# Two unused tiles ahead of the left-hand pools: a shift of SBUF addresses in a three-part attention, expert and convolution kernel

## The chip, the cores and the metric

The kernel runs on one core of a Trainium2 chip. The metric is the device time of one launch in microseconds. TensorE (PE) runs at one of two clock levels, 1.2 or 2.4 GHz; the profile gives the granted share of the higher one. All matrix products here are float32 data; the large ones use the float32r type, in which an operand is split into a high and a low part and a product is the sum of three (high by high, high by low, low by high).

## The reference

Three layers follow each other: a local and global attention, a mixture of experts whose expert is chosen per token (and may be held over from the token before), and a gated network with a three-tap convolution along the sequence.

```python
# attention, B=4, H=8, 512 local + 32 global tokens, head 64, window 32
s_g = scale * q_g @ k_all.T;  out_g = softmax(s_g) @ v_all
s_ll = where(|i - j| <= 32, scale * q_l @ k_l.T, -1e9)
out_l = softmax(concat(scale * q_l @ k_g.T, s_ll)) @ concat(v_g, v_l)
x = concat(out_g, out_l)            # (4, 544, 512)
# experts, E=8, D=512, F=1024
for b, s:
    e = argmax(x @ w_gate) if local_gate < 0.5 or s == 0 else prev_e
    out[b, s] = softmax(x @ w_gate)[e] * (relu(x[b, s] @ w1[e]) @ w2[e])
# second network
h = relu(x @ w_in)
conv_out = sum over k of conv_w[k] * h shifted by k - 1
y = (h * sigmoid(conv_out)) @ w_out
```

## The kernel before, in words

**Stages.** `Attn.run` computes the attention of the four batches (0 to about 150 us of the profile). `Routing` turns the gate logits into lists of tokens: each *slot* holds up to 128 tokens of one expert. `Moe.run` works through the slots (about 147 to 435 us): `gather` fetches the token rows (`xs`, [128, 512]) by an indirect DMA, `turn_x` transposes them and splits them into `xh` and `xl`, `layer1` multiplies them with the first weights, `turn_h` transposes the result and splits it into `gh` and `gl` ([128, 8, 128] each), `layer2` multiplies those with the second weights, and `scatter` writes the rows out. `Ffn2.run` is the second network (about 435 us to the end): 32 units of one batch and one 128-wide slice of the hidden layer, with the second product of a batch issued between the units of the next one, and that of the last batch at the very end.

**Which operand stands and which moves.** In the trace's names `out<-moving,stationary`. In the experts' first product (`l1_mm`, L1112) the token tile `xh` or `xl` is stationary (128 columns, loaded anew for each matmul) and the weights `wh` or `wl` move, 512 columns at a time. In the second (`l2_mm`, L1128) `gh` or `gl` is stationary and the second weights move, 512 columns. In the second network's first product (`l1_half`, L1546) it is the other way round: the weights stand, and the tokens (`f_x0h`/`f_x0l` for batches 0 and 2, `fxh`/`fxl` for 1 and 3) move, 272 columns. In its second (`Ffn2.l2_mm`, L1623) the hidden tile `fh` or `fl` stands and `w_out` moves, 512 columns, 256 in the last tile:

```python
for n, (x, w) in enumerate(((gh, wh), (gh, wl), (gl, wh))):
    self.nc.tensor.matmul(yp[:, cs], x[:, c], w[:, cs], ...)   # L1623: x stands, w moves
```

Every matmul has its own weight load (6066 of each in the profile). The next one's load runs beside the matmul before it.

**Where tiles lie.** SBUF tiles get their addresses in the order in which pools are opened. Pools open from the left (low addresses) unless they say `side="right"`. The first left pool is `const`, opened in `moe_kernel`; it holds `wz`, `ident`, `wcat`, `warm`, `L`, then the routing's tiles. All other left pools follow behind it, each at the place where the pool before it ends: the attention's, then `f_xp` (`fx`, `f_x0h`, `f_x0l`), `w_y` (`ws1`), `m_tp` (`ys`, `gh`, `gl`, `xh`, `xl`, `hs`, `xs`), `w_f` (`wf1`, `wf2`). When the experts are done, `Ffn2.open` opens `f_tp` where `w_y` began: three `f_hp` tiles, then `fxh`, `fxl`, `fc`, `fg`, `fh`, `fl`, `fy`. On the right lie the even batches' attention operands (`kT0`, `qT0`, `VA0`, `VB0`, `VC0`) and later the staging tile `ws2` and the split weights `wh`, `wl` of both layers (`w_hl`). Slots 0 and 1 are gathered before the attention ends, into a right-hand pool (`m_xa`), and slot 0's `xh` and `xl` lie there too.

No order table or planner is involved: the order of instructions is the order in which the code issues them, and it doesn't depend on addresses.

Of the kernel before, what the change touches and what calls it, by code (L numbers as in the profile page):

```python
# [8 lines left out]
F32 = mybir.dt.float32  # L9
# [8 lines left out]
P = 128  # L18
# [69 lines left out]
class Attn:  # L88
    def __init__(self, ctx, cr, cs, tc, q_l, k_l, v_l, q_g, k_g, v_g, wcat, wz, ident, x_dram, L, late, hook):
        self.tc, self.nc = tc, tc.nc  # L90
        nc = tc.nc
        self.q_l, self.k_l, self.v_l, self.q_g, self.k_g, self.v_g = q_l, k_l, v_l, q_g, k_g, v_g
        self.wcat, self.ident, self.x_dram, self.L, self.late, self.hook = wcat, ident, x_dram, L, late, hook
        self.lgt, self.wz = {}, wz
# [247 lines left out]
    def evac(self, c, ps, tag, w=P):  # L342
# [4 lines left out]
        if c < B:  # L347
            j = 4 * c + c // 2
            nc.vector.tensor_copy(self.L[:, j:j + 4, :], t.rearrange("p (i e) -> p i e", e=32)[:, :, 0:9])
        else:  # L350
            nc.vector.tensor_copy(self.L[0:w, 8, :], t[0:w, 0:9])

# [303 lines left out]
class Routing:  # L656
    def __init__(self, nc, c, pool, ident, L):
        self.nc, self.c, self.ident, self.L = nc, c, ident, L
        self.m = pool.tile([P, NT], F32, name="r_m")
# [277 lines left out]
    def few(self, b0, first):  # L937
# [3 lines left out]
        v.scalar_tensor_tensor(sm, b0, -128.0, first[0:1], ALU.mult, ALU.add)  # L941
        v.tensor_scalar(sm, sm, P - TS - 0.5, 1024.0, ALU.is_lt, ALU.mult)
        v.tensor_tensor(sm, sm, b0, ALU.add)
# [39 lines left out]
        v.tensor_tensor(self.gate, pg, rx, ALU.mult)  # L983


TS = 32
NTS = P // TS
NWARM_M = 10
# [66 lines left out]
class Moe:  # L1055
# [8 lines left out]
    def open(self, ctx):  # L1064
        self.ctx = ctx
        self.tp = ctx.enter_context(self.tc.tile_pool(name="m_tp", bufs=2))
        self.ps = ctx.enter_context(self.tc.tile_pool(name="m_ps", bufs=2, space=PSUM))
        self.ys = [self.tp.tile([P, DM], F32, name=f"ys{i}", bufs=1) for i in range(2)]
# [244 lines left out]
    def turn_x(self, s):  # L1313
# [13 lines left out]
        def raw():  # L1327
            nc.scalar.copy(xs[:, 0:NKC * TS].rearrange("p (k t) -> p k t", t=TS), t[:, :, P - TS:P])

# [11 lines left out]
    def layer1(self, s):  # L1341
# [4 lines left out]
        def few():  # L1346
            w = FF // NTS
            for k in range(NKC):
                for j in range(NTS):
                    nc.tensor.matmul(hp[0][TS * j:TS * j + TS, 0:w], xs[:, TS * k:TS * k + TS], W.s[1][:, k, w * j:w * j + w],  # L1350
                                     start=k == 0, stop=k == NKC - 1)
# [31 lines left out]
    def layer2(self, s):  # L1383
# [5 lines left out]
        def few():  # L1389
            for k in range(NFC):  # L1390
                j, a = divmod(k, n)
                for i in range(NTS):
                    nc.tensor.matmul(yp[TS * i:TS * i + TS, 0:w], hs[:, P * (n + a) + TS * j:P * (n + a) + TS * j + TS],
                                     W.s[2][:, k, w * i:w * i + w], start=k == 0, stop=k == NFC - 1)
            for i in range(NTS):
                nc.scalar.copy(y[P - TS:P, w * i:w * i + w], yp[TS * i:TS * i + TS, 0:w])

# [52 lines left out]
class Ffn2:  # L1450
# [32 lines left out]
    def open(self, ctx):  # L1483
        nc, tc = self.nc, self.tc
        self.tp = ctx.enter_context(tc.tile_pool(name="f_tp", bufs=2, reuse_waits="tile"))
        self.ps = ctx.enter_context(tc.tile_pool(name="f_ps", bufs=2, space=PSUM, reuse_waits="tile"))
        self.hp = [self.tp.tile([P, S + 2], F32, name=f"f_hp{i}", bufs=1) for i in range(3)]
        for t in self.hp:
            nc.gpsimd.memset(t[:, 0:1], 0.0)
            nc.gpsimd.memset(t[:, S + 1:S + 2], 0.0)  # L1490
        self.n = 0
# [207 lines left out]
def moe_kernel(ctx, tc, q_l, k_l, v_l, q_g, k_g, v_g, w_gate, w_local, w1, w2, w_in, conv_w, w_out, out):  # L1699
    nc = tc.nc  # L1700
    outf = out.rearrange("b s d -> (b s) d")
    with tc.manual_schedule():
        cp = ctx.enter_context(tc.tile_pool(name="const", bufs=1))
# [8 lines left out]
        warm = cp.tile([P, 1], F32, name="warm")  # L1712
        nc.scalar.activation(warm, ident[:, 0:1], AF.Exp)
        L = cp.tile([P, NT, 9], F32, name="L")
        cc = Consts()

        def late():
# [142 lines left out]
```

## Time and profile before

| | us |
|---|---|
| three runs | 642.68, 645.39, 645.6 (median 645.39) |
| the profiled execution, its own time | 643.43 |
| its span, first to last instruction | 641.7 |
| mean granted clock | 0.984 |

| engine | busy us | share of the span | instructions |
|---|---|---|---|
| PE matmul | 585.6 | 91% | 6066 |
| PE weight load | 483.6 | 75% | 6066 |
| DVE | 415.3 | 65% | 870 |
| ACT | 319.3 | 50% | 634 |
| POOL | 171.3 | 27% | 226 |

DMA moved 90.57 MB. Busy time of PE counts a matmul from its start to its modelled end, which overlaps the next one's start; how fast matmuls follow each other is read from the starts in the timeline, or from a chain piece's length divided by its count.

### The profile page before, as it was taken

The page shows a single profiled execution, that of the slowest core. Times are in us where ns is not written, and L with a number is a line of the kernel's source. Part 1 is how long each engine was busy: PE and PEld are TensorE (multiplying, and loading weights), DVE is VectorE, ACT ScalarE, POOL GpSimd, SP SyncE. Part 2 cuts the span into 40 slices and gives each one's busy share as a digit, 9 for nine tenths or more (in the row PEclk, how much of TensorE's full clock was granted, in tenths as well). Part 3 has the DMA queues.
Part 4 walks back from the last instruction along what each step waited for, and adds up shares of the span by engine and source line. Part 5 has one row for each costly group of instructions (what it writes and reads, how often), then busy time and mean ns, then how long its engine had stood idle before and what let it go on. Part 6 is the DMA issues. An engine that isn't in the chain of part 4 may idle for free. (4 is left out here: it accounts for less than half of the span.)

```text
span 641.7 us, 16204 instructions
## 1 busy us (share of the span) xinstructions
PE 585.6 (91%) x6066; PEld 483.6 (75%) x6066; DVE 415.3 (65%) x870; ACT 319.3 (50%) x634; POOL 171.3 (27%) x226
## 2 busy tenths in 40 slices
PE   7888888888988999979989899978899999999997
PEld 6666666766666888758767678758898998998986
DVE  7867577866956857785596984586983293393340
ACT  4754555564225454552454643665864374363331
POOL 7664910042032223223224230100032132300100
PEclk8999899999999999999999999998899999999999
DMA  8999658658047666575275673123101201000001
GB/s 223 217 218 235 186 126 189 194 194 287 18 158 272 218 210 227 185 264 197 84 261 182 247 281 125 51 89 86 50 1 51 81 3 49 34 1 34 33 35 50
DMA packets 60644, 90.57 MB, mean 141 GB/s; under 512 B 25726, under 2 KB 34198, under 8 KB 60504
## 3 DMA queue, kind: packets, MB, share of 16 engines
q1 hardware_dynamic: 57016, 78.93, 39.7%
q0 software_dynamic: 3520, 10.23, 4.7%
q8 instruction: 64, 1.05, 0.7%
q14 instruction: 44, 0.36, 0.2%
HBM read 125.87 MB, written 15.79 MB: 221 GB/s over the span
## 5 line engine op out<-in xcount | busy, mean ns | idle before, releaser
L1565 DVE SCALAR_TENSOR_TENSOR fc<-f_hp,cw,fc 128x544 f32<-128x544 f32 (+2 forms) x66 | 51.7, 784 | 72.8 <-ACT fc L1563 71.4
L1048 DVE TENSOR_TENSOR wl<-ws,wh 128x512 fp32r<-128x512 f32 (+1 forms) x92 | 74.4, 871 | 14.1 <-ACT wh L1047 12.5
L1047 ACT CAST wh<-ws 128x512 fp32r<-128x512 f32 (+1 forms) x96 | 66.2, 768 | 5.7 <-DMA ws<-in_moe_w_dram 5.3
L1128 PE MATMUL yp<-wl,gh 128*128 128x512 f32 x144 | 57.5, 399 | 3.6 <-DVEq L1299 3.3
L1128 PE MATMUL yp<-wh,gh 128*128 128x512 f32 x144 | 59.2, 411 | 1.1 <-ACTq L1299 0.9
L1128 PE MATMUL yp<-wh,gl 128*128 128x512 f32 x144 | 57.2, 397 | 0.0
L1112 PE MATMUL hp<-wl,xh 128*128 128x512 f32 x144 | 48.6, 409 | 7.7 <-DVEq L1299 7.1
L1623 PE MATMUL f<-wh,fh 128*128 128x512 f32 (+1 forms) x144 | 55.4, 385 | 0.0
L1623 PE MATMUL f<-wl,fh 128*128 128x512 f32 (+1 forms) x144 | 55.1, 383 | 0.0
L1623 PE MATMUL f<-wh,fl 128*128 128x512 f32 (+1 forms) x144 | 55.1, 382 | 0.0
L1112 PE MATMUL hp<-wh,xh 128*128 128x512 f32 x144 | 50.2, 421 | 2.8 <-ACT wh L1047 2.7
L278 ACT ACTIVATE pr<-sp,nm 128x128 f32<-128x128 f32 x128 | 36.5, 374 | 26.2 <-DVE nm L275 26.2
L1276 ACT ACTIVATE hs<-hp 128x512 f32<-128x512 f32 x36 | 19.9, 595 | 59.4 <-PE hp L1112 59.3
L1020 POOL TENSOR_TENSOR wf<-wf,fx 128x512 int32<-128x512 int32 x16 | 20.8, 1300 | 103.1 <-DVE fx L1019 75.3
L1112 PE MATMUL hp<-wh,xl 128*128 128x512 f32 x144 | 47.8, 404 | 0.0
L1073 POOL DMA_INDIRECT xs<-x_dram,gidx x22 | 26.3, 1194 | 73.6 <-ACT pr L278 34.1
L1085 POOL DMA_INDIRECT y_dram<-ys,sidx x22 | 23.6, 1070 | 70.9 <-ACT ys L1401 31.9
L1112 PEld LDWEIGHTS hp<-wl,xh 128*128 128x128 f32 x144 | 27.4, 194 | 16.8 <-DVEq L1299 9.3
L1570 ACT ACTIVATE f_hp<-f 128x544 f32<-128x544 f32 x31 | 19.4, 624 | 35.9 <-PE f L1546 35.7
L1128 PEld LDWEIGHTS yp<-wl,gh 128*128 128x128 f32 x144 | 27.2, 189 | 10.4 <-DVEq L1299 4.2
L1105 DVE TENSOR_TENSOR gl<-hlp,gh 128x512 fp32r<-128x512 f32 x36 | 23.3, 686 | 18.0 <-ACT gh L1378 16.3
L1632 ACT COPY fy<-f 128x512 f32<-128x512 f32 (+1 forms) x18 | 10.1, 563 | 48.6 <-PE f L1623 48.6
(382 smaller groups left out, 1506.3 us busy)
## 6 DMA issues: line engine op xcount, KB each, us to landing
ws<-in_moe_w_dram SPq DMA_DIRECT2D x42, 2048.0 KB
fx<-y_dram SPq DMA_DIRECT2D x17, 256.0 KB
raw<-in_k_l_dram SPq DMA_DIRECT2D x16, 256.0 KB
x_dram<-x SPq DMA_DIRECT2D x16, 256.0 KB
fx<-in_moe_w_in_dram SPq DMA_DIRECT2D x8, 512.0 KB
fx<-in_moe_w_out_dram SPq DMA_DIRECT2D x8, 512.0 KB
out_dram<-fy SPq DMA_DIRECT2D x16, 256.0 KB
VA<-in_v_l_dram SPq DMA_DIRECT2D x20, 192.0 KB
```

Source lines behind the costliest of these rows:

```text
L278: nc.scalar.activation(pr[:, hp, :], sp[:, hp, :], AF.Exp, bias=nm[:, hp:hp + 1], scale=-1.0)
L1020: nc.gpsimd.tensor_tensor(a, a, lo, ALU.add)
L1047: (cp.tensor_copy if cp else self.nc.scalar.copy)(h, src[n][:, k, :])
L1048: eng.tensor_tensor(l, src[n][:, k, :], h.bitcast(F32), ALU.subtract)
L1073: self.nc.gpsimd.indirect_dma_start(out=xs, out_offset=None, in_=self.x_dram[0:n, :], in_offset=bass.IndirectOffsetOnAxis(ap=self.rt.gidx[ ...
L1085: self.nc.gpsimd.indirect_dma_start(out=self.y_dram[:, :], out_offset=bass.IndirectOffsetOnAxis(ap=self.rt.sidx[:, s:s + 1], axis=0), in_= ...
L1105: self.nc.vector.tensor_tensor(hl[1][:, a:a + 4], t, hl[0][:, a:a + 4].bitcast(F32), ALU.subtract)
L1112: self.nc.tensor.matmul(hp[c], a[:, k, :], b[:, 512 * c:512 * c + 512], start=k == 0 and m == 0, stop=k == NKC - 1 and m == 2)
L1128: self.nc.tensor.matmul(yp, a[:, k, :], b, start=k == 0 and m == 0, stop=k == NFC - 1 and m == 2)
L1276: self.nc.scalar.activation(hs[:, 512 * c:512 * c + 512], hp[c], AF.Relu)
L1565: nc.vector.scalar_tensor_tensor(c[:, a:b], hp[:, a + t:b + t], self.cw[:, t, f:f + 1], c[:, a:b], ALU.mult, ALU.add)
L1623: self.nc.tensor.matmul(yp[:, cs], x[:, c], w[:, cs], start=f == 0 and n == 0, stop=f == NFC - 1 and n == 2)
```

## The change

Two tiles are allocated that nothing reads or writes. `pad_c` (104 float32, 416 bytes in each partition) stands in the `const` pool behind `L`, so everything that comes after it on the left moves up by 416 bytes. `pad_f` (8 float32, 32 bytes) is the first tile of `f_tp`, so that pool's other tiles move up by 448. Nothing on the right moves, nor do `ident`, `wz`, `wcat`, `warm` and `L`.

```diff
+PAD_C, PAD_F = 104, 8
...
         self.ps = ctx.enter_context(tc.tile_pool(name="f_ps", bufs=2, space=PSUM, reuse_waits="tile"))
+        self.tp.tile([P, PAD_F], F32, name="pad_f", bufs=1)
         self.hp = [self.tp.tile([P, S + 2], F32, name=f"f_hp{i}", bufs=1) for i in range(3)]
...
         L = cp.tile([P, NT, 9], F32, name="L")
+        cp.tile([P, PAD_C], F32, name="pad_c")
```

The built program has the same instructions in the same order on every engine, with the same waits: only addresses differ. Starting addresses modulo 256, from the two built programs:

| tiles | before | after |
|---|---|---|
| `wh`, `wl` of both layers, `ws2`; `xs` of slots 0 and 1, slot 0's `xh`, `xl` | 224 | 224 |
| `xs`, `xh`, `xl` of the other slots; `gh`, `gl`, `hs`, `ys` of all | 64 | 224 |
| `ws1`, `wf1`, `wf2`, `fx`, `f_x0h`, `f_x0l` | 64 | 224 |
| `fxh`, `fxl`, `fh`, `fl`, `fy` | 32 | 224 |
| `fc`, `fg` (two buffers each) | 32, 160 | 224, 96 |
| `f_hp` (three) | 64, 224, 128 | 0, 160, 64 |
| attention, right: `kT0`, `qT0`, `VA0` / `VB0` / `VC0` | 192 / 128 / 32 | the same |
| attention, left: `kT1`, `qT1`, `VA1` / `VB1` / `VC1` | 32 / 224 / 128 | 192 / 128 / 32 |
| attention, left: `pr`, `pts` | 160 | 64 |
| `ident` | 128 | 128 |

The pieces of a tile that one matmul reads keep its residue, except in `f_x0` and `fx`: a row of their four is 2176 bytes, so an odd row lies 128 further, and the second half of 272 columns 64 further. Their eight pieces lie, seen from the weights that stand, at 96, 160, 224 and 32 (`f_x0`) and at 64, 128, 192 and 0 (`fx`) before; at 0, 64, 128 and 192 for both after. For the tiles that stand before the moving weights, the distance from the stationary tile to the weights is 160 (L1112 but for slot 0, L1128) and 192 (L1623) before, and 0 after.

## Rows read from the trace of the kernel before

**Rows 1.** Busy time by stretch: engines, granted clock, DMA share, GB/s.
```profile
core 0: us, PE busy (x) PEld busy (x) DVE busy (x) ACT busy (x) POOL busy (x), PEclk, DMA share, GB/s
30.00:60.00 30.00, 24.14 (x667) 19.14 (x671) 20.35 (x55) 15.15 (x42) 17.35 (x18) 1.00 0.89 220
...
220.00:260.00 40.00, 40.00 (x192) 32.71 (x191) 27.71 (x46) 18.41 (x32) 11.55 (x10) 1.00 0.53 185
260.00:300.00 40.00, 35.90 (x245) 27.93 (x243) 27.93 (x45) 17.47 (x33) 10.89 (x10) 0.96 0.67 237
```

**Rows 2.** The chain that ended last: start us, us, what (the second network).
```profile
481.61 3.02 PE f L1546 x24
...
493.73 5.59 PE f L1623 x24
...
521.49 2.99 PE f L1546 x24
...
609.82 27.86 PE f L1623 x144
```

**Rows 3.** PE's groups by line and form: count, busy us, mean ns.
```profile
L1128 PE MATMUL yp<-wh,gh 128*128 128x512 f32 x144 | 59.2, 411 | 1.1 <-ACTq L1299 0.9 <-ACT gh L1101 0.2
...
L1623 PE MATMUL f<-wh,fh 128*128 128x512 f32 x128 | 51.0, 398 | 0.0
...
L1112 PE MATMUL hp<-wh,xh 128*128 128x512 f32 x144 | 50.2, 421 | 2.8 <-ACT wh L1047 2.7
...
L1546 PE MATMUL f<-f_x0h,wh 128*128 128x272 f32 x128 | 28.9, 303 | 3.5 <-PEq L1199 3.5
...
L1623 PE MATMUL f<-wh,fh 128*128 128x256 f32 x16 | 4.4, 277 | 0.0
```

**Rows 4.** Timeline of PE, a later slot's second product after a break: start us, us.
```profile
245.04 0.39 PE L1128 MATMUL yp<-wl,gh 128*128 128x512 f32 x1
...
245.96 0.40 PE L1128 MATMUL yp<-wh,gl 128*128 128x512 f32 x1
...
249.95 0.40 PE L1128 MATMUL yp<-wl,gh 128*128 128x512 f32 x1
```

**Rows 5.** Timeline of PE, a stretch at the lower clock.
```profile
288.91 1.06 PE L1112 MATMUL hp<-wh,xl 128*128 128x512 f32 x2
289.76 1.06 PE L1112 MATMUL hp<-wh,xh 128*128 128x512 f32 x2
```

**Rows 6.** Timeline of PE, slot 0's first product, two runs without a break.
```profile
147.30 0.39 PE L1112 MATMUL hp<-wl,xh 128*128 128x512 f32 x1
...
148.22 0.39 PE L1112 MATMUL hp<-wh,xl 128*128 128x512 f32 x1
...
156.98 0.40 PE L1112 MATMUL hp<-wl,xh 128*128 128x512 f32 x1
...
157.91 0.40 PE L1112 MATMUL hp<-wh,xl 128*128 128x512 f32 x1
```

**Rows 7.** Timeline of PE, the last tile's matmuls of 256 columns.
```profile
632.17 0.28 PE L1623 MATMUL f<-wl,fh 128*128 128x256 f32 x1
...
633.99 0.28 PE L1623 MATMUL f<-wh,fl 128*128 128x256 f32 x1
```

**Rows 8.** DVE's groups by form, and min/median/max ns of the `ws` tile's instructions.
```profile
L1048 DVE TENSOR_TENSOR wl<-ws,wh 128x512 fp32r<-128x512 f32 x64 | 42.0, 718 | 7.1 <-ACT wh L1047 5.6 <-PE hp L1112 1.5
...
L1048 DVE TENSOR_TENSOR wl<-wf,wh 128x512 fp32r<-128x512 f32 x8 | 5.3, 690 | 2.8 <-ACT wh L1047 2.6
...
L1048 DVE TENSOR_TENSOR wl<-ws,wh x92: 676/686/1443, 150.8 to 423.8; 128x512 fp32r<-128x512 f32 x64, 128x1024 fp32r<-128x1024 f32 x28
```

**Rows 9.** PE's groups by form: the attention's products with V.
```profile
L300 PE MATMUL op<-VC,pts 128*32 128x65 f32 x384 | 21.5, 223 | 1.3 <-ACT pr L278 1.3
...
L300 PE MATMUL op<-VB,pts 128*32 128x65 f32 x320 | 21.2, 223 | 2.8 <-issue 2.7
```

## The prediction

> **What bounds the kernel now.** I read the stretches first. In the experts' stage a stretch such as 220 to 260 us has PE busy for all of its 40.00 us at a granted clock of 1.00, beside DVE at 27.71, ACT at 18.41 and DMA at 0.53 [rows 1]; in the attention, 30 to 60 us, PE is busy for 24.14 of 30.00 and DMA for 0.89 of the time [rows 1]. Then the chain that ended last: through the second network it consists of PE alone, pieces of 24 matmuls one behind the other, down to the last piece of 144 matmuls that takes 27.86 us [rows 2]. So from the experts on, the end moves with the time from one matmul's start to the next one's, which I call the step. The change adds no instruction and no wait; it can act only through what an instruction costs at another address, and above all through the step of the large matmuls.
>
> The step now. Second network, second product: 5.59 us for 24, so 233 ns for 512 columns [rows 2]. Experts, second product: 245.96 to 249.95 us holds 17 steps, 235 ns each [rows 4]; I use 234. At the lower clock, 1.2 GHz, two matmuls of 512 columns take 289.76 - 288.91 = 0.85 us, or 425 ns each, one column for each clock period [rows 5]. At 2.4 GHz the same would be half, 213 ns. So at full clock every large matmul is stretched by some 20 ns, about 10%, and it is this stretch that an address could act on. The Trainium skill (TensorE: Matmul & The Clock Gate, section on the 56 ns gap) gives a step of N / 2.4 + 2.5 ns, 215.7 for 512 columns. The trace doesn't agree: its step is 233 to 234 ns.
>
> **The change, part by part.** *Two allocations*: no instruction, 0 us.
>
> *Experts' products, stationary tile from distance 160 to distance 0.* L1112 and L1128 have three forms of 144 rows each, 864 matmuls [rows 3]; 24 of L1112 belong to slot 0, whose `xh` and `xl` already lie at distance 0. So 840 move. Slot 0 is the experiment that the kernel before holds by chance: where it runs without a break, four steps take 148.22 - 147.30 = 0.92 us (230 ns) and 157.91 - 156.98 = 0.93 us (232 ns) [rows 6]. A later slot's first four steps after a break, at distance 160, take 245.96 - 245.04 = 0.92 us, 230 ns [rows 4]. Like for like the two distances don't differ by more than the reading of 0.01 us in four steps, 2 to 3 ns. The other neighbour is L1623, distance 192, with its 233 against 234. I take 233 for distance 0, since it is the longer series: 840 x -1 ns = -0.8 us. Bounds: below, the least stretch that a full-clock row of this kind shows, the 256-column matmuls of the last tile, 633.99 - 632.17 = 1.82 us for 16, 114 ns, or 227.5 for 512 columns [rows 7]: -6.5 ns x 840 = -5.5 us. Above, the largest difference that two sets of addresses show in one line, the next item's 1%: +2.3 ns x 840 = +1.9 us.
>
> *Second network, second product, 192 to 0.* 384 matmuls of 512 columns and 48 of 256 (three forms of 128 and of 16) [rows 3]. I take no change, for slot 0's reason. Bounds: -5.5 ns x 384 = -2.1 us, and +2.3 x 384 = +0.9 us.
>
> *Second network, first product.* Six forms of 128 rows [rows 3], half with `f_x0`, half with `fx`. The pieces of `fx` lie at 64, 128, 192 and 0 from the weights and step 3.02 us / 24 = 126 ns; those of `f_x0` lie at odd multiples of 32 and step 2.99 / 24 = 124.6 ns [rows 2]. That is 1.25 ns, 1%. After the change both lie at multiples of 64. `fx` keeps its set: 0. `f_x0` should step like `fx`: 384 x 1.25 ns = +0.5 us. Bounds 0 and +0.5.
>
> *Everything else at a new address.* DVE's subtraction L1048 reads two SBUF tiles. With `ws2` and `wh` at equal residues (the rows with 512 columns) it takes 718 ns on the mean, but 676 at the least and 686 in the middle of all forms; with `wf2`, 96 bytes off, 690 [rows 8]. So equal residues cost nothing there, the mean being drawn up by a few long ones, and DVE has 12 us to spare in 40 [rows 1]. If each of the 12 `wf` subtractions lost 28 ns it would be 0.3 us. In the attention `pts` moves against `VA0`, `VB0`, `VC0`, not against `VA1`, `VB1`, `VC1`; the products with `VC` and `VB`, which lie at 32, 128 and 224, all take 223 ns on the mean [rows 9]. I cost it at 0; the cover is PE's own 6 us of idle time in 30 [rows 1], and without cover 1% of 24 us for each 30 us would be 1.2 us over the stage. Transfers into shifted tiles keep their size and number; DMA's idle half in the experts' stage covers them.
>
> Sum: -0.8 + 0 + 0.5 + 0 = -0.3 us. The profiled execution took 643.43 us (span 641.7), 2 us under the median of 645.39; the four times average 644.3. An unchanged kernel lands there, so the forecast is 644.3 - 0.3 = **644.0 us**. The sum on the profiled execution itself would be 643.1.
>
> **Rivals.** *The addresses matter fully (faster).* Two readers, the moving operand and the next weight load, get in each other's way, and equal residues keep them apart. For it: the stretch exists only at the higher clock, and it differs between 256 and 512 columns, so it isn't a fixed cost. Against it: slot 0. If the step fell to twice that of 256 columns, both bounds below together give 5.5 + 2.1 = 7.6 us: 636.7 us. Chance 0.17. If the whole stretch went, 21 ns x 840 + 20 ns x 384 = 25 us would go: 619 us. Slot 0's 230 to 232 ns all but excludes that; chance 0.03. By the skill's formula above, 215.7 ns, it would be 22 us, an estimate.
>
> *Equal residues collide (slower).* Stationary and moving operand now begin at the same place modulo 256, so each matmul could start with the two readers at the same spot, in every matmul from 160 us on. For it: `fx`, whose set holds 0, steps 1% longer than `f_x0`. Price: 2.3 ns x 1224 + 0.5 us = +3.3 us, 647.6 us; it decides from 2.6 ns a matmul on, since 2.6 x 1224 is 3.2 us. Against it again: slot 0. Chance 0.14.
>
> *Addresses don't matter at all.* The tiles are where the title says, so the change is real, but the differences of 1 ns may come from the rhythm of the instructions around them. For it speaks the same 223 ns at the three residues of V. Against it, that `fx` and `f_x0` differ in every piece of the chain. Then 644.3 us. The skill says so too (same page, section on the phases of a matmul): loading the next weights doesn't take read bandwidth from the running matmul, by which no shift of either is worth anything. The trace can't show which of the two readers makes the stretch. Chance 0.26; the forecast itself, with its terms of 1 ns, 0.40.
>
> **How the numbers follow.** Runs of this kernel differ by 642.68 to 645.6, and a stretch at the lower clock costs: 260 to 300 us has 0.96 [rows 1], 1.6 us of full clock lost. Such stretches may come or go by chance. Under 0.5%, 3.2 us, a measurement can't tell a change from none. The range takes the forecast with that scatter, all of the collision's price (647.6) above, and some 4.5 us of the gain below, which is a little over half of the first rival's: 639.5 to 648.0. Outside lie the full gains and a collision worse than any row shows. Faster by over 0.5%: 0.17 + 0.03 = 0.20; within: 0.40 + 0.26 = 0.66; slower: 0.14.
>
> **What would show it.** In the changed profile: 24 matmuls of L1623 in 5.5 to 5.65 us, a step of 232 to 235 ns in L1112 and L1128, and the 24 matmuls of L1546 with `f_x0` at 3.02 instead of 2.99 us. A step of 228 or less in L1128 or L1623 makes the forecast wrong towards faster, one of 237 or more towards slower. Steps as before with another time would mean that something outside PE's stream answers to addresses, DVE's L1048 or the attention's stage first.

## The result and the profile after

| | before | after |
|---|---|---|
| median of five runs each, us | 644.13 (641.71 to 645.6) | 638.0 (636.7 to 638.52) |
| the profiled execution, its own time (span), us | 643.43 (641.7) | 636.7 (634.9) |
| mean granted clock | 0.984 | 0.985 |

The ratio is 0.9906, 95% interval 0.9876 to 0.9935: faster by 0.9%, 6.1 us. The forecast was 644.0 us with a range from 639.5; the result lies 1.5 us below that range.

In the changed kernel the lines of `Moe` stand one further down (L1112 is L1113, L1128 is L1129), those of `Ffn2` two (L1546 is L1548, L1623 is L1625). I go back to the views in which the prediction looked for the step. First the chain that ended last (start us, us, what), for [rows 2]:

```profile
541.86 3.01 PE f L1548 x24
...
566.48 5.46 PE f L1625 x24
...
603.40 27.55 PE f L1625 x144
```

24 matmuls of the second product take 5.46 us where they took 5.59, 227.5 ns a step instead of 233. The last piece, which holds all the 256-column matmuls of batch 3 as well, gains less: 27.55 for 27.86. The 24 of the first product with `f_x0` (the piece at 541.86) take 3.01 for 2.99, a little more than before.

The experts, timeline of PE (start us, us), a second product after a break, for [rows 4]:

```profile
230.69 0.48 PE L1129 MATMUL yp<-wh,gh 128*128 128x512 f32 x1
231.00 0.40 PE L1129 MATMUL yp<-wl,gh 128*128 128x512 f32 x1
...
231.93 0.40 PE L1129 MATMUL yp<-wh,gl 128*128 128x512 f32 x1
...
233.08 0.39 PE L1129 MATMUL yp<-wl,gh 128*128 128x512 f32 x1
...
235.80 0.39 PE L1129 MATMUL yp<-wl,gh 128*128 128x512 f32 x1
...
625.14 0.28 PE L1625 MATMUL f<-wl,fh 128*128 128x256 f32 x1
...
625.74 0.28 PE L1625 MATMUL f<-wh,fh 128*128 128x256 f32 x1
```

Read this in three pieces. The first four steps after the break, 231.00 to 231.93, take 0.93 us, 232 ns: what [rows 4] and [rows 6] showed before. The twelve from 233.08 to 235.80 take 2.72 us, 226.7 ns. So a series begins as before and settles, after about eight steps, at something faster. The last two rows are the 256-column matmuls, for [rows 7]: 0.60 us for five, 120 ns, where they took 114. These got slower.

The mean of all steps inside unbroken series at the higher clock, worked out from the starts in both traces:

```text
                              before    after   (ns)
L1112/L1113, 512 columns      234.2     228.5
L1128/L1129, 512 columns      234.0     228.4
L1623/L1625, 512 columns      233.2     227.6
L1623/L1625, 256 columns      113.4     119.8
L1546/L1548, f_x0             124.6     125.4
L1546/L1548, fx               125.5     125.5
from the 13th step of a series on: 234.4 -> 226.7, 234.3 -> 226.7, 233.4 -> 226.7 (first three lines)
```

Counted up: 840 x 5.6 = 4.7 us and 384 x 5.6 = 2.1 us gained, 48 x 6.4 = 0.3 us and 384 x 0.8 = 0.3 us lost, together 6.2 us. The measured difference of the medians is 6.1.

That agreement is better than it deserves, as the stages of the two profiled executions show:

```text
                                            before   after  (us)
start to the first L1112                    147.0    144.4
from there to the last L1128                283.3    281.9
from the first L1546 to the last L1623      202.5    199.6
```

2.6 us come from the attention, which takes 142.2 to 147.4 us in the profiles of this study: 145.1 on the mean of the five in which its addresses are those of the kernel before, 144.9 of the seven in which they are those of the changed one modulo 256. That part is chance as far as can be told. The second network's 2.9 us are in part chance too: over all profiles it takes 199.9 us on the mean of seven with `fh` and `fl` at distance 0 and 201.2 of the six at 32, 128 and 192, 1.3 us less, where the steps count 2.1 - 0.3 - 0.3 = 1.5. And the experts' stage gives 1.4 us instead of 4.7. The stretches (columns as in [rows 1]) and PE's waits in the experts' stage (who waits for whom: us, times, longest) tell where the rest went:

```profile
220.00:260.00 40.00, 40.00 (x196) 33.24 (x195) 29.29 (x48) 17.53 (x31) 10.56 (x10) 1.00 0.54 189
260.00:300.00 40.00, 35.93 (x247) 28.31 (x246) 27.40 (x44) 18.47 (x34) 13.05 (x11) 0.96 0.72 244
```

```profile
PE hp L1113 <- DVEq L1300: 7.4, 5, 3.2
PE hp L1113 <- ACT wh L1048: 3.3, 2, 2.2
PE hp L1113 <- DVE wl L1049: 0.9, 2, 0.5
```

Where PE has no break (220 to 260) it does 196 matmuls in the time of 192 [rows 1], 2% more. Where it waits (260 to 300) it does 247 for 245: a faster PE reaches the next slot's operands earlier and waits for them. The same three waits of the kernel before:

```profile
PE hp L1112 <- DVEq L1299: 7.1, 5, 3.3
PE hp L1112 <- ACT wh L1047: 2.7, 2, 2.1
PE hp L1112 <- DVE wl L1048: 0.5, 1, 0.5
```

They are 1.3 us longer now: part of the gain is spent waiting for the copies on ACT and DVE and for DVE's queue at L1300. In the sum over the stage, time in unbroken series at the higher clock fell from 180.4 to 174.2 us, stretches of over 0.7 us between two starts rose from 28.4 to 29.7 (over all profiles, 27.1 on the mean at other distances and 28.7 at 0), and more steps were taken at the lower clock, 21 for 12 (22 and 16 on the mean), where the step stays what it was [rows 5]:

```profile
285.14 1.05 PE L1113 MATMUL hp<-wh,xh 128*128 128x512 f32 x2
286.00 1.05 PE L1113 MATMUL hp<-wl,xh 128*128 128x512 f32 x2
286.85 1.05 PE L1113 MATMUL hp<-wh,xl 128*128 128x512 f32 x2
```

Four matmuls from 285.14 to 286.85 are 428 ns each (timeline of PE). Over all profiles of this study the experts' stage takes 282.3 us on the mean of eight at distance 0 (281.2 to 284.2), 284.0 of seven at others (282.3 to 286.1): of 4.7 us about 1.7 is seen to arrive. The means account for the rest: 1.6 us more in the long stretches, and 6 more steps at the lower clock, at some 0.2 us each, make about 1.3 us.

### The profile page after: what moved, and what is told of

The parts are those of the page before. It is cut to its first block, busy times and chain, and to the rows that moved or that the text cites. A ratio compares the mean times of both kernels' runs of the same rounds, so it can differ in the third digit from the quotient of the medians.

```text
span 634.9 us, 16204 instructions
## 1 busy us (share of the span) xinstructions
PE 579.0 (91%) x6066; PEld 481.3 (76%) x6066; DVE 414.3 (65%) x870; ACT 319.4 (50%) x634; POOL 171.9 (27%) x226
## 5 line engine op out<-in xcount | busy, mean ns | idle before, releaser
L1129 PE MATMUL yp<-wl,gh 128*128 128x512 f32 x144 | 57.5, 399 | 3.7 <-DVEq L1300 3.3
L1129 PE MATMUL yp<-wh,gh 128*128 128x512 f32 x144 | 58.8, 408 | 1.1 <-ACTq L1300 0.9
L1129 PE MATMUL yp<-wh,gl 128*128 128x512 f32 x144 | 57.2, 398 | 0.0
L1113 PE MATMUL hp<-wl,xh 128*128 128x512 f32 x144 | 47.7, 403 | 8.2 <-DVEq L1300 7.4
L1625 PE MATMUL f<-wh,fh 128*128 128x512 f32 (+1 forms) x144 | 54.8, 380 | 0.0
L1625 PE MATMUL f<-wh,fl 128*128 128x512 f32 (+1 forms) x144 | 54.5, 378 | 0.0
L1625 PE MATMUL f<-wl,fh 128*128 128x512 f32 (+1 forms) x144 | 54.4, 378 | 0.0
L1113 PE MATMUL hp<-wh,xh 128*128 128x512 f32 x144 | 49.4, 414 | 3.4 <-ACT wh L1048 3.3
L278 ACT ACTIVATE pr<-sp,nm 128x128 f32<-128x128 f32 x128 | 36.5, 374 | 27.1 <-DVE nm L275 27.0
L1113 PE MATMUL hp<-wh,xl 128*128 128x512 f32 x144 | 47.3, 400 | 0.0
L1113 PEld LDWEIGHTS hp<-wl,xh 128*128 128x128 f32 x144 | 27.0, 192 | 16.9 <-DVEq L1300 9.5
L1129 PEld LDWEIGHTS yp<-wl,gh 128*128 128x128 f32 x144 | 27.4, 190 | 10.3 <-DVEq L1300 4.3
L1402 ACT COPY ys<-yp 128x512 f32<-128x512 f32 x15 | 8.8, 587 | 50.0 <-PE yp L1129 47.0
```

The costliest lines, as they stand in the source:

```text
L278: nc.scalar.activation(pr[:, hp, :], sp[:, hp, :], AF.Exp, bias=nm[:, hp:hp + 1], scale=-1.0)
L1113: self.nc.tensor.matmul(hp[c], a[:, k, :], b[:, 512 * c:512 * c + 512], start=k == 0 and m == 0, stop=k == NKC - 1 and m == 2)
L1129: self.nc.tensor.matmul(yp, a[:, k, :], b, start=k == 0 and m == 0, stop=k == NFC - 1 and m == 2)
L1625: self.nc.tensor.matmul(yp[:, cs], x[:, c], w[:, cs], start=f == 0 and n == 0, stop=f == NFC - 1 and n == 2)
```

## The experiments

The theory that stood after the result: the step of a float32r matmul with a weight load beside it, 128 columns standing and 512 moving, depends on the distance from the standing tile to the moving weights modulo 256, and on nothing else of the address. Against it stood an effect of the absolute address, another period (512), another bearer of the gain (one of the two products alone, or the attention), and, later, two readings of what the distance is: E, in which the standing tile acts while it is loaded, that is beside the matmul before its own, and F, in which it acts in its own matmul. Edits are given against the changed kernel unless it says otherwise.

**1. The experts alone.**

```diff
-PAD_C, PAD_F = 104, 8
+PAD_C, PAD_F = 104, 24
```

This puts `fh`, `fl` and `fxh`, `fxl` back at 32.

> Only the experts' tiles move to distance 0 from the weights; the second tile is made longer (24 float32), so that the second network's tiles keep their old residue of 32. Theory A (the distance between the standing tile and the moving weights, modulo 256, sets the step that a long unbroken series of matmuls settles to): L1112 and L1128 settle at 227 ns, L1623 stays at 233, and 840 x about 5.6 ns = 4.7 us of the gain are there: about 639.5 us where the kernel before takes 644. Rival B (the gain lies in the second network alone, where the chain is PE from end to end, and the experts' gain is lost in waits): under 1 us. Rival C (the gain is chance, fewer stretches at the lower clock): the steps of before.

Measured: 640.45 us (ten runs) against 642.6 (25 runs of the kernel before on the same chip), ratio 0.9951 (0.9908 to 0.9994). Its timeline of PE in the experts and its chain in the second network:

```profile
248.01 0.39 PE L1129 MATMUL yp<-wh,gh 128*128 128x512 f32 x1
...
251.18 0.39 PE L1129 MATMUL yp<-wh,gl 128*128 128x512 f32 x1
```

```profile
597.86 5.59 PE f L1625 x24
609.49 27.86 PE f L1625 x144
```

14 steps from 248.01 take 3.17 us, 226.4 ns; the second network is as it was to the last digit.

**2. The hidden tile of the second network alone.**

```diff
-PAD_C, PAD_F = 104, 8
+PAD_F = 48
...
-        cp.tile([P, PAD_C], F32, name="pad_c")
```

> No tile in the const pool; a tile of 48 float32 ahead of the second network's tiles, so that its h lies at distance 0 and the experts' tiles at 160 as before. Theory A: L1623 with 512 columns settles at 227 ns (2.1 us less over 384), its 48 matmuls of 256 columns go from 113 to 120 ns (0.3 us more), L1112 and L1128 stay at 234; some 1.8 us less, about 642. Rival B: 5 us less. Rival C: steps of before.

Measured: 640.2 us (ten runs), ratio 0.997 (0.9937 to 1.0003). The same two views:

```profile
246.91 0.40 PE L1129 MATMUL yp<-wh,gh 128*128 128x512 f32 x1
...
250.19 0.40 PE L1129 MATMUL yp<-wh,gl 128*128 128x512 f32 x1
```

```profile
594.20 5.46 PE f L1625 x24
605.69 27.55 PE f L1625 x144
```

Now the 14 steps take 3.28 us, 234.3 ns, and the second network has the changed kernel's pieces. So each half of the change moves the step of its own products and no other's. The times agree with both halves counting (-2.2 and -2.4 us), but their intervals are as wide as what they tell: the steps carry the verdict, not the times.

**3. The weights moved instead of the tiles that stand** (against the kernel before; `xh`, `gh` stay at 64, `fh` comes to 64, and the split weights come to 64 instead of 224).

```diff
+        hl.tile([P, 40], F32, name="pad_w")
...
+        self.tp.tile([P, 8], F32, name="pad_f", bufs=1)
```

> The weights come to the rows instead: an unused tile of 160 bytes behind the split weights moves these and the staging tile on the right down, so that they lie at 64 modulo 256, where the experts' tiles lie; 32 bytes ahead of the second network's tiles bring those to 64 as well. Nothing else on the left moves. Theory A (only the distance counts): steps of 227 ns in L1112, L1128 and L1623, 638 us as with the change. Rival D (the place of the rows counts by itself, 64 against 224, or their start within 64 bytes): the steps of before, 234 and 233, and 644 us.

Measured: 637.85 us (ten runs), ratio 0.9926 (0.9892 to 0.996). Steps 228.1 and 228.8 in the experts, 227.5 in the second network, and in its chain:

```profile
591.13 5.46 PE f L1626 x24
602.63 27.55 PE f L1626 x144
```

Standing tiles and weights lie at 64 here and at 224 in the changed kernel, only the distance is the same: the absolute address is out.

**4. Distance 0 modulo 256, 256 modulo 512.**

```diff
-PAD_C, PAD_F = 104, 8
+PAD_C, PAD_F = 40, 8
```

> As the change, with the const tile shorter by 256 bytes (40 float32). All distances are the same modulo 256, but where the change has 256 modulo 512 between standing tile and weights, this has 0. Theory A with a period of 256 or less: steps of 227 ns and the change's time. With a period of 512 or more: other steps, as much as several ns away.

Measured in one run: 641.27 us (642.6 before). One run says nothing on the time, since runs of the kernel before go from 636.95 to 646.19 in that comparison; steps 228.7 and 228.5, and the chain's pieces:

```profile
596.47 5.46 PE f L1625 x24
607.97 27.55 PE f L1625 x144
```

The period is not 512.

**5 to 7. Other distances.** In the order of the three labels below (128 and 64: the experts' and the second network's distance):

```diff
-PAD_C, PAD_F = 104, 8
+PAD_C, PAD_F = 8, 24
+PAD_C, PAD_F = 16, 24
+PAD_C, PAD_F = 48, 32
```

> Distance from standing tile to moving weights 128 in the experts and 64 in the second network's second product. Theory A1 (two readers meet at a spot that repeats every 256 bytes): 128 and 64 are not the meeting point that 0 is; steps near 233 to 234 ns, or a value of their own. Theory A2 (the period is 128): the experts settle at 227 ns as with 0, and 64 behaves like 192, 233 ns. Theory A3 (only 0 differs, by accident of a start): all others 233 to 234.

> Distances 96 in the experts and 32 in the second network's second product. A1: a step of its own for each, 227 to 235 ns; neighbours of 0 like 32 may lie lower or higher than 227. A2 (period 128): 32 behaves like 160, 234 ns.

> Distances 224 in the experts and 128 in the second network's second product. A1: a step of its own for each; 128 the same here as in the experts of the run with 128 and 64, although line, stage and neighbours differ. A2 (period 128): 128 settles at 227 ns, 224 is like 96.

Measured: 639.66, 641.41 and 638.93 us, one run each (638.47 before, one run too, so the times tell nothing). Chains of the three, in this order:

```profile
594.79 5.50 PE f L1625 x24
```

```profile
596.03 5.60 PE f L1625 x24
```

```profile
593.48 5.59 PE f L1625 x24
```

In steps: 128, 96 and 224 give the experts 232.7, 233.3 and 233.2 ns. In the second network 64 gives 229, 32 gives 233.2 and 128 gives 232.9. Between 0 and the rest there is no slope towards 0, but a plateau at 233 with a few exceptions. The 256-column matmuls take 117.8, 116.7 and 118.7 ns, against 113.4 at distance 192 and 119.8 at 0: their order is another one.

**8. One of the three parts at another distance**: `fl` at 192, `fh` at 0.

```diff
+            if x == "l" and self.first:
+                self.tp.tile([P, 16], F32, name="pad_l", bufs=1)
+                self.first = False
```

> As the change, but 64 bytes between the high and the low parts of the second network's h: fh stays at distance 0, fl goes to 192. Of each three matmuls the third (weights high, fl standing) has the far tile as its own standing tile, and the second (weights low, fh standing) is the one beside which fl is loaded. Theory E (the stretch is the moving read against the next weight load, which runs beside it): the second of three changes. Theory F (a matmul's own standing tile matters): the third. If the steps only settle in a long regular series, all three lie between 227 and 233. The experts stay at 227.

Measured: 636.75 us, one run. Settled steps by place among the three: 228.4 (`wh` against `fh`), 229.2 (`wl` against `fh`), 235.6 (`wh` against `fl`). `fl` is loaded during the second and used in the third, and the third is long, as F has it. The mean, 231.1, lies between the two distances. Experiment 13 shows why this reading was too quick.

**9. A sweep behind the kernel's end** (against the kernel before). Series of 32 equal matmuls follow the second network. One slice of `f_x0h` stands, starting `o` float32 later from series to series, and a tile of `w_out` moves; the distance is 160 - 4 `o`, modulo 256. Nobody uses what they compute.

```diff
+def sweep(nc, f2):
+    x, w = f2.x0[0], f2.w2[0][0]
...
+    def series(o, m, n):
+        mark()
+        p = f2.y_tile()
+        for _ in range(SERIES):
+            nc.tensor.matmul(p[0:m, 0:n], x[:, 0, o:o + m], w[:, 0:n], start=True, stop=True)
...
+    for o in range(0, 64, 4):
+        series(o, P, 512)
```

> The kernel before, with series of 32 equal matmuls behind the end, whose results go nowhere: one high-part tile stands (a slice of it that starts later and later in its row), one w_out tile moves. Distances from standing to moving in steps of 16 bytes over 256, with 512, 256 and 272 columns moving; then 64 and 32 standing columns at eight distances; then steps of 4 bytes around distance 0, and slices 256 and 512 bytes further at distance 0. Its time is not compared. Theory A: the step of 512 columns repeats what the kernels showed: 227 ns at 0, 233 at 32, 96, 128, 192 and 224, 229 at 64, 234 at 160; the slices at 256 and 512 bytes step like 0; 256 columns: 120 at 0, 113 at 192. Theory E (the stretch comes from the next weight load that runs beside the matmul): with 64 standing columns the stretch over 213 ns is about half, with 32 a quarter of what 128 have. Theory G (the stretch comes from the moving read or the result alone): the same stretch with 64 and 32 columns.

The whole took 1068.94 us, which is not compared. Its timeline has one row for a series (start us, length of 32); the rows shown are the distances 160, 64, 32, 16, 0, 240 and 192, then 160 with 256 columns, and at the end 160 and 0 with 64 standing columns:

```profile
637.73 7.76 PE L1712 MATMUL f<-wh,f_x0h 128*128 128x512 f32 x32
...
684.38 7.61 PE L1712 MATMUL f<-wh,f_x0h 128*128 128x512 f32 x32
...
699.83 7.71 PE L1712 MATMUL f<-wh,f_x0h 128*128 128x512 f32 x32
707.60 7.58 PE L1712 MATMUL f<-wh,f_x0h 128*128 128x512 f32 x32
715.24 7.55 PE L1712 MATMUL f<-wh,f_x0h 128*128 128x512 f32 x32
722.85 7.74 PE L1712 MATMUL f<-wh,f_x0h 128*128 128x512 f32 x32
...
746.23 7.73 PE L1712 MATMUL f<-wh,f_x0h 128*128 128x512 f32 x32
...
761.77 4.02 PE L1712 MATMUL f<-wh,f_x0h 128*128 128x256 f32 x32
...
897.03 7.47 PE L1712 MATMUL f<-wh,f_x0h 128*64 128x512 f32 x32
...
935.13 7.58 PE L1712 MATMUL f<-wh,f_x0h 128*64 128x512 f32 x32
```

The mean of the last 16 steps of each series, from the starts:

```text
distance    0     16    32    48    64    80    96   112   128   144   160   176   192 to 240
ns        226.7 228.3 233.3 233.3 229.1 230.0 233.2 233.3 232.9 233.4 234.3 232.2 233.3
distance   +4 226.7    +8 233.4    -4 232.4    -8 230.6
distance 0, slice 256 and 512 bytes further: 226.6, 226.7
256 columns: 116.6 to 120.0 (0 and 112 the slowest)    272 columns: 123.3 to 126.8
standing columns, 512 moving, at distance   0     32    64    96    128   160   192   224
64 standing                               229.7 230.8 228.3 230.9 231.3 226.7 232.6 231.8
32 standing                               231.6 233.4 231.6 233.4 231.1 230.9 230.8 240.0
```

Four things come out of it. The period is 256. Distance 0 is, with 4, the best for 512 columns and, with 112, the worst for 256. The good step is sharp: 8 bytes lose it. And the number of standing columns changes which distance is good: with 64 it is 160 (226.7), the worst with 128, and 0 has 229.7. On the mean of these eight distances 128, 64 and 32 standing columns take 232.0, 230.3 and 232.9 ns, so the stretch isn't in proportion to what the load reads. For 256 columns the distance isn't all: at 192 the sweep, with one slice standing throughout, has 117.8 ns where the kernel, with three parts in turn, has 113.4.

**10. The rows of the tokens 2304 bytes long**, so that all eight pieces of `fx` and `f_x0` share one residue but for the second half of 272 columns.

```diff
-PAD_C, PAD_F = 104, 8
+PAD_C, PAD_F, PAD_S = 40, 8, 32
...
-        self.x0 = [xp.tile([P, 4, S], F32R, name=f"f_x0{i}") for i in "hl"]
+        self.x0 = [xp.tile([P, 4, S + PAD_S], F32R, name=f"f_x0{i}") for i in "hl"]
```

(and the same for `fxh`, `fxl`)

> As the change, with rows of the second network's x made 2304 bytes long (32 unused float32 at the end of each), so that of the moving pieces of L1546 all four rows lie alike: the first half of 272 columns at 0 from the standing weights, the second at 64. The const tile is 40 float32 here, the same modulo 256. Theory A with the distance as the only cause: the step of L1546 leaves 125.4 ns, by up to 5 ns either way as 256 columns did between distances (113 to 120), 768 x 5 ns = 3.8 us at most; the other steps stay at 227. Theory H (272 columns never settle, since two halves at different distances alternate): 125 ns as before.

Measured: 637.14 us, one run (643.59 before). In its chain L1548 takes 3.02 us, so 126 ns: no gain at the first product.

```profile
589.32 3.02 PE f L1548 x24
592.34 5.45 PE f L1625 x24
603.82 27.57 PE f L1625 x144
```

**11 and 12. A version meant to beat the change, beside the change itself.** The tokens of the second network go to odd multiples of 32 from the weights, where `f_x0` had its 124.6 ns, and everything else to distance 0.

```diff
-PAD_C, PAD_F = 104, 8
+PAD_C, PAD_X, PAD_Y, PAD_F, PAD_H = 40, 8, 56, 16, 56
...
+        xp.tile([P, PAD_X], F32, name="pad_x")
         self.x0 = [xp.tile([P, 4, S], F32R, name=f"f_x0{i}") for i in "hl"]
...
+        xp.tile([P, PAD_Y], F32, name="pad_y")
...
+            self.tp.tile([P, PAD_H], F32, name="pad_h", bufs=1)
```

> As the change, with the second network's x, the moving operand of L1546, at odd multiples of 32 bytes from the standing weights in all its pieces, as half of it had before (unused tiles of 32 bytes ahead of f_x0 and of fxh, and of 224 bytes behind, so that all other tiles keep residue 224). Theory A: L1546 steps at 124.5 ns instead of 125.4, 768 x 0.9 ns = 0.7 us less than the change; everything else as with the change. Theory H (the step of 272 columns depends on more than that distance): 125 ns, no gain.

> The change itself once more, for the size of its gain. Counted from steps alone: 840 x 5.6 ns + 384 x 5.6 ns - 48 x 6.4 ns - 384 x 0.8 ns = 4.7 + 2.1 - 0.3 - 0.3 = 6.2 us less, ratio 0.990. If the experts' stage gives back part in waits for the split weights, as its length in the profiles suggests (about 282 us with distance 0, about 284 without), some 3.5 to 4 us less, 0.994 to 0.995.

Measured on one chip, six runs each, against 643.23 us (eleven runs): 635.74, ratio 0.9894 (0.9861 to 0.9927), and for the change 636.62, ratio 0.9886 (0.9854 to 0.9919). The change's gain is there a second time, 6.6 us by the medians. The other version cannot be told from it, and its first product is not faster but slower, 126 ns:

```profile
587.79 3.03 PE f L1550 x24
590.82 5.49 PE f L1630 x24
```

So "odd multiples of 32 are good for 272 columns", which I had read out of [rows 2], does not hold. Experiments 6 and 7 had shown it already, where all pieces lie at odd multiples too: 125.7 and 125.9 ns with `f_x0`. Which residues the eight pieces have doesn't set the cost of a matmul of 272 columns; their order may, as the same four begin at 160 in the kernel before (124.5) and at 224 here and in experiment 7 (126.0, 125.9), but no run tries it by itself, and nothing here gives a rule. No version of this study beats the change.

**13. One matmul put out of step** (against the kernel before). Behind the end stand series of 72 matmuls at distance 0; from the 15th on, one of every 14, called k, has its standing slice, its moving columns or both shifted by 32, 64, 96 or 160 bytes; in a fourth way the moving columns of k and the standing slice of k + 1 are shifted together.

```diff
+            a = 40 + (still.get(k, 0) if i >= 14 else 0)
+            b = moving.get(k, 0) if i >= 14 else 0
+            nc.tensor.matmul(p, x[:, 0, a:a + P], w[:, b:b + 512], start=True, stop=True)
...
+        series({4: d}, {})
+        series({}, {4: d})
+        series({4: d}, {4: d})
+        series({5: d}, {4: d})
```

> The kernel before, with series of 72 matmuls of 512 columns behind the end, all at distance 0, in which from the fifteenth on one of every fourteen (number k) is put out of step by 32, 64, 96 or 160 bytes in one of four ways. Steps are counted from a settled 227 ns. Theory E (the moving read of a matmul meets the load of the next one's standing tile, which runs beside it): (1) standing tile of k shifted: the step of k-1 changes first; (2) moving tile of k shifted: step k changes; (3) both of k shifted: steps k-1 and k change; (4) moving of k and standing of k+1 shifted together: no step changes. Theory F (a matmul's own two operands): (1) and (2) step k, (3) none, (4) k and k+1. If the addresses count only through the rhythm of the whole series, a pulse in any way lengthens several steps behind it as after a break (233, 236, 224, 231, 236, 228, 232, 231) without a rule on where it begins.

Steps worked out from the starts in the trace, in ns, beginning with the step of k - 1. The settled step is 227, and the pattern returns from period to period to within about 1 ns:

```text
shift 32 bytes
standing of k          235 228 232 231 227
moving of k            227 236 233 233 236 224 231 236 228 232 231 227
both of k              235 230 232 232 231 227
moving k, stand k+1    227 236 230 236 228 232 231 227
shift 96 bytes
standing of k          228 231 236 228 233 230 227
moving of k            227 236 230 236 228 233 231 227
both of k              229 234 234 233 230 227
moving k, stand k+1    227 231 231 231 236 228 233 231 227
first two steps (k - 1, k), shift      32        64        96       160
standing of k                       235 228   226 236   228 231   237 232
moving of k                         227 236   227 236   227 236   227 234
both of k                           235 230   226 232   229 234   237 232
moving k, stand k+1                 227 236   227 232   227 231   226 233
```

A standing slice that is shifted by 32 or 160 bytes changes the step before its own (235 and 237 for 227), while it is being loaded, which F can't give: F falls. At 96 bytes that step changes by 1 ns, at 64 not at all, although a series that lies at these distances throughout settles at 233 to 234 (experiment 9). Moving columns change their own step and leave the one before alone, at all four shifts. So E has the place right where the change shows, but not its size. In the fourth way, the distance between the two that run together is 0 all the time, E expects nothing, and the step of k grows all the same, by 4 to 9 ns. Any jump costs, and three to eleven steps pass until the rhythm is back. This also explains experiment 8: at 64 bytes the step beside the load is 226 and the long one, 236, comes after it, so a place in a cycle of three doesn't show where the cause acts.

## Why the prediction was wrong

**What bounds the kernel, and where an address can act.** Right: through the step of the large matmuls, and through nothing else that could be found. DVE's subtraction takes 683 ns in the middle (686 before).

**The experts' term, -0.8 us.** This is the step that failed: "Like for like the two distances don't differ by more than the reading of 0.01 us in four steps." The sentence is true, and the changed profile repeats it (232 ns in the first four steps). What it cannot bear is the conclusion. Slot 0's series have at most five steps and lie wholly inside the first eight steps after a break, in which either distance gives about 232 ns. From then on one settles at 226.7 and the other at 234. By position after a break, after the change: 232.8, 234.2, 228.4, 229.8, 233.0, 229.0, 230.0, 229.3, then 226.7; before: 232.6, 232.7, 232.7, 232.3, 236.5, 237.3, 231.8, 233.7, then 234.3. Slot 0's own first product, whose distance is 0 in both kernels, takes 231.8 ns before and 231.6 after. The term was mis-sized: -4.7 us of PE's own time instead of -0.8, though within its bound of -5.5.

**The second product of the second network, 0 us.** Wrong by the same step: -5.6 ns x 384 = -2.1 us, at the end of its bound. The 48 matmuls of 256 columns went the other way, +6.4 ns each, +0.3 us; I had put them into the same item without a price of their own.

**The first product, +0.5 us.** Right in sign: 3.01 us for the 24 with `f_x0` where 3.02 was forecast, 0.8 ns instead of 1.25, so +0.3 us. The reason I gave for it, the set of residues, fell in experiments 6, 7, 10 and 11.

**Everything else, 0 us.** Nothing in the runs speaks against it; the attention's stage varies by more, from profile to profile, than any effect of this size.

**The rival that came true.** "The addresses matter fully" had 636.7 us and a chance of 0.17; the runs gave 638.0. But its bound, twice the step of 256 columns, hit by accident: those matmuls at distance 192 have nothing to do with 512 columns at distance 0, as they became slower at the same distance. Its mechanism, equal residues keep two readers apart, is not shown: half of it holds (the tile that is loaded can act on the matmul beside it), the other half fails in the fourth way of experiment 13, and with 64 standing columns the good distance is 160, not 0. The rival "addresses don't matter" leaned on the Trainium skill (TensorE: Matmul & The Clock Gate, section on the phases of a matmul), by which loading the next weights takes no read bandwidth from the running matmul. The trace doesn't agree with what I drew from it, that no shift is worth anything: shifting nothing but the tile that is being loaded changes the step beside it from 227 to 235 ns at 32 bytes and to 237 at 160 (not at 64). "Equal residues collide" fell for 512 columns; for 256 the step did grow at distance 0, by 6.4 ns.

**What stays open.** What the reads meet in, why 256 and 272 columns and 64 standing columns have an order of their own, and why the fourth way of experiment 13 costs anything. Also open is how much of the 6.2 us counted in steps reaches the end: the stages over all profiles show about 3 us (1.7 in the experts, 1.3 in the second network), the runs 6.1 and 6.6 us, and 4.75 in experiment 3, which has the same distances, and waits and stretches at the lower clock change from run to run by as much as the difference.

## What to carry to other kernels

Take the price of a matmul from a long series without a break, look where its rhythm settles, and don't set a short series against a long one, nor two short ones against each other for what long ones do. Where every matmul of 512 columns loads its own tile of 128 columns, an unused tile that gives the standing operand and the moving one the same address modulo 256 can be worth 3% of each step (234.3 to 226.7 ns here); another number of moving or standing columns has to be measured anew. Series of sliding slices behind the kernel's end measure all distances in one run, but check them in the kernel itself: for 256 columns the two differed (117.8 and 113.4 ns at distance 192). Part of what the bounding engine gains in this way goes into its next wait and into steps at the lower clock, so count these along with the steps.

## What the runs showed of the hardware that was not expected

- A settled step of 512 columns, with 128 standing, is 226.7 ns at distance 0 and 233.3 at most others: 272 and 280 periods of 1.2 GHz. At the lower clock the step is 426.7 ns before and after, 512 periods of 1.2 GHz, so there is no stretch at either distance; half of it would be 213.3 ns or 256 periods.
- The settling: after a break about eight steps of 224 to 241 ns pass in the kernel before a series settles at distance 0, and after a jump of an address three to eleven (experiment 13), in an order that returns from one period to the next to within about 1 ns. It isn't always so: the series at distance 4 in the sweep runs at 226 to 227 ns from its second step on.
- 4 bytes of distance keep the good step (226.7), 8 lose it (233.4), and -4 loses most of it (232.4).
- With 64 standing columns the shortest step, 226.7 ns, is at distance 160, where 128 standing columns have their longest, 234.3; 32 standing columns give 230.8 to 240.0 ns.
